# Turned keys and state products of six blocks from one TensorE pass, with every engine's order rewritten

## The chip, the cores and the metric

The kernel runs on one core of a Trainium2 chip. That core has TensorE (PE in the profile: matrix products into PSUM, eight banks of 128 partitions by 512 float32), VectorE (DVE), ScalarE (ACT), GpSimd (POOL, which here mostly starts loads) and SyncE (SP, which starts stores and a few loads). Each engine works through its own instructions in order and waits on semaphores for the others. The metric is the device time of the kernel in microseconds.

## The reference

A linear attention with a decayed state feeds a channel mix. Sizes: batch 4, heads 8, sequence 768, head width 64, so d_model 512; hidden width 1024.

```python
for t in range(S):                       # attention, state is 64x64 for each head
    state = gamma * state + k[t] v[t]^T
    y[t] = scale * q[t] state
x = y, heads side by side                # (4, 768, 512)
x_prev = x, one token later (zeros first)
xk = mu_k * x + (1 - mu_k) * x_prev
xr = mu_r * x + (1 - mu_r) * x_prev
k = relu(xk @ w_k); v = k*k @ w_v        # 512 -> 1024 -> 512
out = sigmoid(xr @ w_r) * v              # w_r is 512x512
```

## The kernel before

The 3072 tokens are cut into 12 blocks of 256 (three to a batch, so blocks 0, 3, 6, 9 begin with an empty state and blocks 2, 5, 8, 11 hand none on). A block's attention is chunked: scores of queries and keys inside the block, a mask, the product with the values, plus the queries times the state carried in. Decay is folded into scale factors of the values and of the output. Blocks 6 to 11 (the tuple HALF, line 17) are cut into four sub-blocks of 64 tokens, so their matmuls are 64x64 tiles of TensorE.

One long string, ORDER, is the program: each word is a piece of work, a number of a block (and more), the PSUM bank after `@` and the engine after `~`. The loop at line 755 emits the words one after the other, and no scheduler changes that. An engine's instructions therefore stand in the order of its own words, and only semaphores tie the engines together. The pieces that matter here, with the lines of the profile:

- `lq`, `lk`, `lv`, `wk`, `wr`, `wv` load (lines 230, 235, 735, 738, 742). Nearly all go through POOL's queue, which casts q, k and the weights to float16. `cq`, `ck` cast the first q and k on ACT (line 241).
- `vs` scales the values to float16 (line 253), on DVE or POOL. The tiles are a ring of three.
- `Tq`, `Tk` turn q and k with transposes against an identity (lines 272 and 278), `Eq`, `Ek` copy the result from PSUM to float16 (line 241, ACT).
- `S` is the scores (lines 318, 331, 339), `M` the masking (lines 347, 354, DVE).
- `C` is the state product k^T v (lines 366, 384, 395), `U` adds it to the carried state (line 419, or a copy at line 241), `G` decays the state into the next block (line 424).
- `I` and `J` are the queries times the carried state (line 441), `Y` the scores times the values (lines 462, 478, 489). All three accumulate in the same PSUM bank pair of a block; `D` scales that into x (lines 507, 514, DVE).
- `t`, `dx`, `X` mix x with its neighbour token (lines 529, 542, 552, 558), `K` is xk times w_k (lines 572, 582), `Qa`, `Qb` relu and square (lines 591, 599, 603, ACT), `R` and `s` the gate and its sigmoid (lines 612, 618), `V`, `O`, `st` the last product, its gating and the store (lines 624, 630, 637). The last half block has its own forms `Vc`, `Oc`, `sc` (lines 642, 649, 657).
- `z` multiplies zeros on TensorE (lines 703, 710) in the start-up.

A key block of 6 to 11 is thus read twice by TensorE before: in `Tk`, 32 transposes of 64 columns into a float16 bank pair, and in `C`, 32 matmuls (24 where no state is handed on) of 64 columns:

```python
nc.tensor.transpose(pt[low(s), u, j, i, :], src[low(u), h, i*D : i*D+D], ident[low(u), low(u)])
nc.tensor.matmul(ps[low(a), u, i, j, :], lhsT=K16(n)[low(u), h, i*D : i*D+D], rhs=VS(n)[low(u), i, h], ...)
```

Of the kernel before, what the change touches and what calls it, by code (L numbers as in the profile page):

```python
# [29 lines left out]
t.0.0.3~a t.0.0.2~a t.0.0.1~a lv.2~p z.2@4 S.1.1@23 M.1.1~v C.1@01 U.1.0~v z.2@4 I.1@23 S.1.0@67  # L30
X.0.0.1~v t.0.1.2~a X.0.0.2~v Tk.2@0 t.0.1.3~a t.0.0.0~a M.1.0~v X.0.0.0~v z.2@4 Y.1 t.0.1.1~a
X.0.0.3~v Ek.2~a K.0.0@0 K.0.1@6 lq.4~p U.1.1~v G.1~a wr~p lk.4~p D.1~v dx.1~v X.1.0.2~v X.1.0.0~v
K.0.2@1 Qa.0.0~a Qb.0.0~a Qa.0.2~a lq.3~p X.1.0.1~v X.1.0.3~v X.1.1.0~v Qa.0.1~a K.0.3@0 Qa.0.3~a
lk.3~p vs.2~v Tq.2@1 X.1.1.2~v K.1.3@6 K.1.0@0 C.2@7 U.2.0~v lv.3~p Eq.2~a S.2.1@23 M.2.1~v S.2.0@45
M.2.0~v Qb.0.3~a lv.4~p K.1.1@1 X.1.1.1~v Qa.1.0~a t.0.1.0~a K.1.2@7 I.2@23 Qb.0.1~a Qa.1.1~a wv.0~p
Qb.0.2~a Tq.4@01 Eq.4~a Y.2 Qa.1.3~a Qb.1.1~a X.0.1.3~v X.1.1.3~v R.1.1@4 Tk.4@01 Ek.4~a J.2 R.1.0@6
Qa.1.2~a s.1.0~a X.0.1.2~v X.0.1.1~v X.0.1.0~v R.0.1@5 s.0.1~a s.1.1~a R.0.0@7 s.0.0~a S.4.1@01
Qb.1.0~a D.2~v dx.2~v X.2.0.2~v X.2.0.0~v S.4.0@23 Tq.3@4 Eq.3~a X.2.0.1~v wv.1~p X.2.0.3~v Tk.3@7
lq.5~p Ek.3~a K.2.2@5 Qa.2.2~a K.2.3@4 M.4.1~v M.4.0~v Qa.2.3~a Qb.2.3~a lk.6~p S.3.1@67 M.3.1~v
S.3.0@01 vs.3~p C.3@23 U.3.0~a Qb.2.2~a K.2.1@4 Qa.2.1~a K.2.0@2 Qa.2.0~a I.3@45 lq.6~p vs.4~v  # L40
C.4@67 U.3.1~v X.2.1.1~v V.0.1.0@3 M.3.0~v V.1.0.0@2 G.3~a U.4.0~v I.4@01 X.2.1.3~v U.4.1~v J.3
Qb.1.3~a Y.4 Qb.2.0~a lk.5~p X.2.1.2~v X.2.1.0~v Y.3 D.3~v dx.3~v V.0.0.0@7 V.0.1.1 O.0.1~v Tq.5@45
J.4 D.4~v dx.4~v R.2.0@6 Qb.2.1~a V.0.0.1 O.0.0~v X.3.0.1~v Eq.5~a Qb.1.2~a V.1.0.1 X.3.0.2~v
O.1.0~v Tq.6@01 Eq.6~a Tk.6@45 Ek.6~a st.0.0~s lk.7~p st.1.0~s V.1.1.0@3 V.1.1.1 O.1.1~v s.2.0~a
R.2.1@0 s.2.1~a lv.5~p X.3.0.0~v X.3.0.3~v Tk.7@67 Ek.7~a G.4~a S.6@45 M.6~v Tk.5@23 Ek.5~a vs.5~v
V.2.0.0@0 K.3.2@1 Qa.3.2~a K.3.0@6 S.5.0@23 M.5.0~v S.5.1@45 C.5@1 U.5.0~v K.3.3@7 Qb.3.2~a Qa.3.0~a
lq.7~p K.3.7@6 Qa.3.3~a Qa.3.7~a lv.6~p lq.8~p vs.6~v M.5.1~v V.2.0.1 st.0.1~s I.5@67 O.2.0~v
st.2.0~s C.6@23 U.6.0~a U.6.1~v U.6.2~v K.3.6@1 Qa.3.6~a lk.9~p X.3.1.3~v Y.5 Tq.7@45 Eq.7~a U.6.3~v
X.3.1.2~v I.6@01 J.5 X.3.1.0~v D.5~v X.3.1.1~v Qb.3.3~a G.6~a V.2.1.0@2 K.3.1@3 V.2.1.1 O.2.1~v
Qb.3.7~a Qa.3.1~a Qb.3.1~a dx.5~v K.3.4@4 K.3.5@5 Qa.3.5~a X.5.0.0~v X.5.0.3~v R.3.1@2 s.3.1~a  # L50
lv.7~p Qa.3.4~a X.5.0.1~v Qb.3.4~a R.3.0@5 R.4.0@2 s.3.0~a s.4.0~a Qb.3.0~a X.5.0.2~v vs.7~v K.5.2@4
S.7@67 st.1.1~s M.7~v Qb.3.5~a Y.6 Qb.3.6~a lv.10~p C.7@23 U.7.0~v X.5.1.1~v Qa.5.2~a K.5.0@5
R.4.1@6 Qa.5.0~a D.6~v s.4.1~a V.4.0.0@4 V.4.0.1 V.3.1.0@5 U.7.1~v Qb.5.0~a X.5.1.3~v U.7.2~v I.7@01
X.5.1.2~v U.7.3~v Tq.8@67 Eq.8~a X.5.1.0~v O.4.0~v lv.8~p vs.8~v Qb.5.2~a lq.10~p lk.8~p Tk.8@23
Ek.8~a V.3.1.1 V.3.0.0@4 C.8@67 O.3.1~v st.2.1~s st.3.1~s Y.7 dx.6~v D.7~v Tq.10@23 V.3.0.1 Eq.10~a
G.7~a dx.7~v X.6.0.2~v V.4.1.0@5 R.5.1@2 s.5.1~a K.5.3@0 Qa.5.3~a R.5.0@2 U.8.0~v O.3.0~v V.4.1.1
lv.9~p lk.10~p lq.9~p Tk.10@01 s.5.0~a U.8.1~v X.6.0.1~v Ek.10~a X.6.0.0~v Tk.9@23 Ek.9~a K.5.1@7
Qa.5.1~a X.6.0.3~v K.6.0@4 lq.11~p Qb.5.1~a Qa.6.0~a U.8.2~v I.8@01 vs.9~v S.8@23 M.8~v O.4.1~v
st.4.1~s K.6.4@7 Qa.6.4~a vs.10~v X.6.1.2~v K.6.2@6 C.9@23 Qa.6.2~a Qb.6.2~a U.9.0~a Y.8 U.9.1~v
D.8~v U.9.2~v U.9.3~v X.6.1.3~v Qb.5.3~a Tq.9@45 V.5.1.0@6 V.5.1.1 O.5.1~v Eq.9~a lk.11~p K.6.3@7  # L60
Qa.6.3~a K.6.7@4 Qa.6.7~a V.5.0.0@7 C.10@45 Qb.6.0~a X.6.1.0~v S.9@23 M.9~v G.9~a Qb.6.3~a Tq.11@01
Eq.11~a V.5.0.1 dx.8~v X.6.1.1~v st.4.0~s K.6.1@6 Qb.6.7~a Qa.6.1~a Qb.6.1~a X.8.0.3~v X.8.0.0~v
U.10.0~v U.10.1~v K.6.5@2 Qa.6.5~a st.3.0~s lv.11~s K.6.6@0 Qa.6.6~a Qb.6.6~a R.6.0@6 s.6.0~a
O.5.0~v U.10.2~v U.10.3~v R.7.0@2 s.7.0~a R.6.1@7 s.6.1~a I.9@45 X.8.0.2~v S.10@23 Tk.11@01 Ek.11~a
X.8.0.1~v K.8.1@7 Qb.6.5~a Qa.8.1~a Qb.8.1~a vs.11~v st.5.1~s K.8.0@6 C.11@01 M.10~v Qb.6.4~a
# [19 lines left out]
def kernel(  # L85
# [114 lines left out]
    def half(n):  # L200
        return n in HALF
# [10 lines left out]
    def first(n):  # L212
        return n % NB == 0
# [586 lines left out]
```

## Time and profile before

| | |
|---|---|
| median of 3 runs | 153.29 us (153.18 to 153.69) |
| span of the profiled execution | 151.4 us, from its first to its last instruction |
| PE busy | 143.4 us, 2426 matmuls |
| DVE busy | 127.8 us, 212 instructions |
| ACT busy | 103.6 us, 195 instructions |
| POOL busy | 55.3 us, 65 instructions |
| granted TensorE clock | 1.000 |

The profiled execution is known by its span; the timed runs count 1.9 us more, which lies around the span. A difference in the span is taken as the same difference in the time. In the view by groups, one row is one line, engine and shape with its count, its busy time and the mean length of one; lengths overlap, since an engine starts an instruction before the one ahead of it has ended, so what an instruction takes of a busy engine is read from one start to the next in the timeline. The chain of waits goes back from the last instruction to what released each step. The view by stretches gives the busy time of each engine between two moments.

### The profile page before, as it was taken

The numbers are of one execution on the slowest core, as the hardware profiler recorded it, in microseconds if no ns is written. First come the engines' busy times: TensorE is split into PE (matmuls) and PEld (weight loads), VectorE is DVE, ScalarE is ACT, GpSimd is POOL, SyncE is SP. The second block draws the span as 40 slices with busy tenths as digits, with TensorE's granted clock in tenths as the row PEclk, the third lists the DMA queues.
The fourth block names the chain that finished last, engine by engine and source line by source line (L and its number), as shares of the span: only waits on it lengthen the run. The fifth ranks groups of instructions, "written<-read, shape, count | busy, mean of one in ns | idle before, by whom it ended". The sixth has DMA issues, their size and how long they took to land.

```text
span 151.4 us, 5541 instructions
## 1 busy us (share of the span) xinstructions
PE 143.4 (95%) x2426; PEld 82.8 (55%) x2426; DVE 127.8 (84%) x212; ACT 103.6 (68%) x195; POOL 55.3 (37%) x65
## 2 busy tenths in 40 slices
PE   7878799999999999999999999999999999999991
PEld 3345487757754554547465564548456444655450
DVE  7886999999989999999999999999799999400432
ACT  3565979899844795779567786999604756839420
POOL 7953998577957309996710000000000000000000
PEclk9999999999999999999999999999999999999999
DMA  5999999999999999999999019301000005500433
GB/s 140 219 229 197 207 231 192 168 251 212 196 167 202 233 262 107 256 300 198 231 173 126 7 38 283 105 35 45 0 4 0 4 0 211 205 0 0 148 133 139
DMA packets 45624, 22.16 MB, mean 146 GB/s; under 512 B 37400, under 2 KB 41248, under 8 KB 45600
## 3 DMA queue, kind: packets, MB, share of 16 engines
q0 software_dynamic: 38704, 14.42, 74.5%
q1 hardware_dynamic: 6592, 7.21, 14.3%
q8 instruction: 19, 0.31, 0.8%
q10 hardware_dynamic: 304, 0.18, 0.4%
q14 instruction: 5, 0.04, 0.1%
HBM read 24.16 MB, written 6.29 MB: 201 GB/s over the span
## 4 chain that ended last, share of the span: by engine, by line
PE 73%; DMA 12%; POOL 11%; issue 1%; DVE 0%; POOLq 0%
PE ps L624 27%; PE ps L572 14%; DMA v<-in_v_dram 12%; PE ps L612 12%; PE ps L582 8%; PE ps L278 3%; POOL q L235 3%; POOL k L230 2%; PE ps L441 2%; POOL vs L253 2%; POOL v L230 2%; PE ps L366 1%; PE ps L462 1%; PE ps L642 1%; PE ps L318 1%
## 5 line engine op out<-in xcount | busy, mean ns | idle before, releaser
L624 PE MATMUL ps<-wv,k2s 128*128 128x512 f16 x184 | 44.1, 380 | 0.0
L591 ACT ACTIVATE kr<-ps 128x512 f32<-128x512 f32 x48 | 27.9, 594 | 12.5 <-PE ps L582 6.5
L624 PEld LDWEIGHTS <-k2s 128*128 128x128 f16 x184 | 17.1, 98 | 18.9 <-ACT k2s L603 0.4
L630 DVE SCALAR_TENSOR_TENSOR os<-ps,rs 128x512 f32<-128x512 f32 x23 | 15.6, 684 | 11.9 <-ACT rs L618 9.4
L612 PE MATMUL ps<-wr,xr 128*128 128x512 f16 x96 | 23.5, 379 | 0.0
L582 PE MATMUL ps<-xk,wk 128*128 128x256 f16 x192 | 23.2, 273 | 0.0
L572 PE MATMUL ps<-xk,wk 128*128 128x512 f16 x96 | 23.0, 379 | 0.0
L618 ACT ACTIVATE rs<-ps 128x512 f32<-128x512 f32 x24 | 13.6, 597 | 12.9 <-PE ps L612 12.1
L230 POOL DMA_DIRECT2D k<-in_k_dram x20 | 17.8, 903 | 10.3 <-PE ps L384 6.7
L582 PEld LDWEIGHTS <-wk 128*128 128x128 f16 x192 | 18.1, 98 | 3.7
L241 ACT COPY qT<-ps 128x1024 f16<-128x1024 f16 (+1 forms) x13 | 12.3, 946 | 9.5 <-PE ps L278 7.8
L558 DVE SCALAR_TENSOR_TENSOR xr<-dx,mu,xT 128x256 f16<-128x256 f32 (+1 forms) x32 | 17.9, 577 | 0.1
L230 POOL DMA_DIRECT2D v<-in_v_dram x18 | 16.0, 911 | 3.6 <-DMA wr<-in_moe_w_r_dram 1.9
L558 DVE SCALAR_TENSOR_TENSOR xk<-dx,mu,xT 128x256 f16<-128x256 f32 (+1 forms) x32 | 17.0, 579 | 0.2
L354 DVE TENSOR_TENSOR a<-ps,c_sb 128x1024 f16<-128x1024 f32 (+1 forms) x14 | 14.6, 1066 | 0.9 <-PE ps L339 0.6
L603 ACT ACTIVATE k2s<-kr 128x512 f16<-128x512 f32 x24 | 14.8, 631 | 0.3
L612 PEld LDWEIGHTS <-xr 128*128 128x128 f16 x96 | 9.0, 97 | 10.7 <-issue 0.5
L572 PEld LDWEIGHTS <-wk 128*128 128x128 f16 x96 | 9.1, 98 | 10.5
L599 ACT ACTIVATE k2s<-kr 128x512 f16<-128x512 f32 x24 | 14.5, 627 | 0.3
L241 ACT COPY kT<-ps 128x1024 f16<-128x1024 f16 (+1 forms) x13 | 12.2, 945 | 2.2 <-PE ps L272 1.7
L529 DVE TENSOR_TENSOR dx<-xT 128x1024 f32<-128x1024 f32 x11 | 13.4, 1221 | 0.2
L253 DVE TENSOR_TENSOR vs<-v,csm_sb 128x1024 f16<-128x1024 f32 x10 | 12.2, 1217 | 0.2 <-DMA v<-in_v_dram 0.2
(73 smaller groups left out, 165.6 us busy)
## 6 DMA issues: line engine op xcount, KB each, us to landing
out_dram<-os SPq DMA_DIRECT2D x23, 256.0 KB, 2.4
v<-in_v_dram POOLq DMA_DIRECT2D x18, 256.0 KB, 7.7
q<-in_q_dram POOLq DMA_DIRECT2D x11, 256.0 KB, 8.4
k<-in_k_dram POOLq DMA_DIRECT2D x21, 128.0 KB, 8.8
v<-in_v_dram POOLq DMA_DIRECT2D x2, 512.0 KB, 7.2
wk<-in_moe_w_k_dram POOLq DMA_DIRECT2D x2, 512.0 KB, 10.4
wv<-in_moe_w_v_dram POOLq DMA_DIRECT2D x2, 512.0 KB, 10.4
wr<-in_moe_w_r_dram POOLq DMA_DIRECT2D x1, 512.0 KB, 8.7
```

What stands on the lines that cost most here:

```text
L230: e.dma_start(out=dst[:, :, i * D : i * D + D], in_=src[:, i * P : i * P + P].rearrange("h p d -> p h d"),)
L241: e.copy(out=out, in_=in_)
L253: e.tensor_tensor(out=VS(n), in0=V32(n).rearrange("p h (i d) -> p i h d", i=2), in1=gks[:, int(half(n) or wide(n)), :, :, None].to_broadca ...
L354: nc.vector.tensor_tensor(out=a_full(n)[:, i, :, j0:j1], in0=pairs(banks("S", n, i, j0))[:, :, j0:j1], in1=(below if wide(n) else causal[: ...
L558: nc.vector.scalar_tensor_tensor(out=XM[w](k)[:, j, t0:t1], in0=DX(k)[:, j, t0:t1], scalar=mu[:, w * NCO + j : w * NCO + j + 1], in1=x[:, ...
L572: nc.tensor.matmul(banks("K", n, g), lhsT=wk16[:, co, g * P : g * P + P], rhs=XM[0](k)[:, co, :], start=(co == 0), stop=(co == NCO - 1),)
L582: nc.tensor.matmul(pz[:, i, :], lhsT=wk16[:, co, fo * P : fo * P + P], rhs=XM[0](k)[:, co, m * TM + t0 : m * TM + t1], start=(i == 0 and c ...
L591: nc.scalar.activation(out=kr, in_=banks("K", n, g, *u), func=AF.Relu)
L603: nc.scalar.activation(out=K2(n)[:, w * g : w * g + w, t0:t1], in_=kr.rearrange("p a t -> p (a t)").rearrange("p (i t) -> p i t", i=w), fu ...
L612: nc.tensor.matmul(banks("R", n, tb), lhsT=XM[1](k)[:, co, t : t + P], rhs=wr16[:, co, :], start=(co == 0), stop=(co == NCO - 1),)
L624: nc.tensor.matmul(banks("V", n, tb), lhsT=K2(n)[:, fo, tb * P : tb * P + P], rhs=wv16[:, fo, :], start=(fo == 0), stop=(fo == NFO - 1),)
L630: nc.vector.scalar_tensor_tensor(out=OS(2 * n + tb), in0=banks("V", n, tb), scalar=1.0 / (KSC * KSC), in1=RS(2 * n + tb), op0=ALU.mult, op ...
```

## The change

For blocks 6 to 11, `Tk`, `Ek` and `C` go. In their place stands `TC`, in two halves `TC.n.0` and `TC.n.1` of 16 matmuls each: the same slice of K is the stationary operand as in `C`, and the moving operand is 128 columns wide, 64 of an identity and 64 of the scaled values. The first 64 columns of the result are the turned keys, the others the state product, both in float32. For that, the tile of scaled values has an identity as its slot 0, written once in the start-up into the three tiles of the ring (three DVE instructions more). `Ec.n.i` copies the turned keys of one half to float16 (ACT, 512 elements of a partition, twice a block; `Ek` was one copy of 1024). `U` reads the state product out of the same banks.

A second new piece, `w`, is a fence: for each of the 12 blocks ACT copies 16 elements of a partition (8 in the first blocks of the whole-block form) out of the bank pair in which `I` has just written. The next matmul that writes there (`J` or `Y`) has to wait for that copy. Before, nothing stood between them.

Besides, the load of w_k is in three pieces (a quarter, a quarter, a half) in place of two halves, the scaling of block 3's values goes from POOL to DVE, the two mu vectors are staged in a tile that also serves output, and ORDER is new throughout, so on every engine and queue pieces stand in other places.

```diff
+MERGED = (6, 7, 8, 9, 10, 11)
 ORDER = """
-cm.0~v cm.1~v cm.2~v gy.0~v mu~a lv.0~p lq.0.0.2~s lk.0.0.2~s ck.0.0.2~a cq.0.0.2~a z.12@6
...
+lq.0.0.2~s cm.0~v mu~a lv.0~p lk.0.0.2~s z.4@2 z.4@3 z.2@2 mt@0 gy.0~v cm.1~v cq.0.0.2~a Tq.0.0.2@1
...
+    def VS(n):
+        return VI(n)[:, 1:].rearrange("p (i h) d -> p i h d", i=2)
+
-    VS = ring("vs_", 3, [2, H, D], F16)
+    VI = ring("vs_", 3, [2 * H + 1, D], F16)
...
-    mu8 = const.tile([P, P], F32, name="mu8")
+    fenced = const.tile([P, 2, NJ, 2], F32, name="fenced")
...
+    mu8 = OS(2)[:, 0:P]
...
+    def both(n, i):
+        return banks("TC", n, i).rearrange("p u (j x t) -> p u j x t", j=NJ, x=2)
+
+    def turned_state(e, n, i):
+        ps = both(n, i)
+        for j in range(NJ):
+            for u in range(2):
+                for a, h, jo, hp in heads(j):
+                    k = 1 + i * H + h
+                    x = slice(0, 2) if more(n) or not (u and i) else slice(0, 1)
+                    nc.tensor.matmul(
+                        ps[low(a), u, j, x], lhsT=K16(n)[low(u), h, i * D : i * D + D],
+                        rhs=VI(n)[low(u), 0 : k + 1 : k][:, x],
+                        start=(j == 0), stop=(j == NJ - 1), skip_group_check=True,
+                    )
+
+    def turned_k_part(e, n, i):
+        copy(
+            e, KT(n)[:, :, i].rearrange("c j (u p) -> c u j p", u=2), both(n, i)[:, :, :, 0],
+        )
...
+        if merged(n):
+            src = both(n, c // 2)[:, c % 2, :, 1]
...
+    def fence(e, n):
+        us = slice(0 if half(n) or not first(n) else 1, 2)
+        e.copy(out=fenced[:, us], in_=pairs(banks("I", n))[:, us, :, 0:C:W])
+
...
-            ((step, 2, ALU.is_ge), (below, 0, ALU.is_ge)),
+            ((step, 2, ALU.is_ge), (below, 0, ALU.is_ge))
+            + tuple((VI(i)[:, 0], 2, ALU.is_equal) for i in range(3) if MERGED),
...
-    def load_wk(e, h):
-        f = slice(h * dff // 2, (h + 1) * dff // 2)
+    def load_wk(e, a, b):
+        f = slice(a * dff // 4, b * dff // 4)
         nc.gpsimd.dma_start(out=wk16[:, :, f], in_=wks[:, :, f])
```

Three places of the new order, on the engines that the prediction speaks of. First DVE in the start-up, from the first scaling of values (tile vs_0) to the first x (tile xT0); a2 is a masked score, tg2 and t32 the carried state. Before:

```order
L253 TENSOR_TENSOR vs_0_74<-v32_0_70,csm_sb_121 128x1024
L354 TENSOR_TENSOR a2_0_83<-ps_61,c16_sb_120 128x2x256
L243 CAST tg2_0_93<-ps_61 128x256
L419 TENSOR_TENSOR t32_0_86<-ps_61,tg2_0_93 128x256
L354 TENSOR_TENSOR a2_0_83<-ps_61,c16_sb_120 128x2x256 x3
L514 TENSOR_TENSOR xT0_130<-ps_61,gy_sb_122 128x2x4x128
```

And now:

```order
L717 TENSOR_SCALAR vs_0_74<-os_3_119,csm_sb_121 128x64
L717 TENSOR_SCALAR vs_1_75<-os_3_119,csm_sb_121 128x64
L717 TENSOR_SCALAR vs_2_76<-os_3_119,csm_sb_121 128x64
L363 TENSOR_TENSOR a2_0_83<-ps_61,c16_sb_120 128x2x256
L262 TENSOR_TENSOR vs_0_74<-v32_0_70,csm_sb_121 128x1024
L363 TENSOR_TENSOR a2_0_83<-ps_61,c16_sb_120 128x2x256
L252 CAST tg2_0_93<-ps_61 128x256
L451 TENSOR_TENSOR t32_0_86<-ps_61,tg2_0_93 128x256
L363 TENSOR_TENSOR a2_0_83<-ps_61,c16_sb_120 128x2x256 x2
L765 TENSOR_TENSOR gy_sb_122<-gy_sb_122,csm_sb_121 128x4x128
L546 TENSOR_TENSOR xT0_130<-ps_61,gy_sb_122 128x2x4x128
```

The three identities are new, one mask stands ahead of the values, and the last power of gy stands behind the masks instead of ahead of the values.

Second, DVE around block 3's values, after the four xk of block 2 (a2 and tg2, t32 as above). Before:

```order
L558 SCALAR_TENSOR_TENSOR xk_2_103<-dx_0_99,mu_125,xT0_130 128x256 x4
L354 TENSOR_TENSOR a2_1_84<-ps_61,c16_sb_120 128x1024 x2
L354 TENSOR_TENSOR a2_0_83<-ps_61,c16_sb_120 128x1024
L253 TENSOR_TENSOR vs_1_75<-v32_0_70,csm_sb_121 128x1024
L419 TENSOR_TENSOR t32_0_86<-ps_61,tg2_0_93 128x256
```

And now:

```order
L594 SCALAR_TENSOR_TENSOR xk_2_103<-dx_0_99,mu_125,xT0_130 128x256 x4
L262 TENSOR_TENSOR vs_0_74<-v32_3_73,csm_sb_121 128x1024
L363 TENSOR_TENSOR a2_0_83<-ps_61,c16_sb_120 128x1024 x2
L451 TENSOR_TENSOR t32_0_86<-ps_61,tg2_0_93 128x256
L262 TENSOR_TENSOR vs_1_75<-v32_0_70,csm_sb_121 128x1024
```

The second row, the values of block 3 (tile vs_0), was POOL's and is DVE's now.

Third, ACT around blocks 9 and 10 (rs is a sigmoid, k2s a square, kr a relu, qT and kT turned queries and keys). Before:

```order
L618 ACTIVATE rs_0_112<-ps_61 128x512
L618 ACTIVATE rs_2_114<-ps_61 128x512
L618 ACTIVATE rs_1_113<-ps_61 128x512
L241 COPY kT_2_82<-ps_61 128x2x8x64
L599 ACTIVATE k2s_111<-kr_2_109 128x2x256
L591 ACTIVATE kr_3_110<-ps_61 128x512
```

And now:

```order
L250 CAST kT_1_81<-ps_61 128x2x4x64
L250 COPY qT_2_79<-ps_61 128x2x4x128
L250 CAST kT_1_81<-ps_61 128x2x4x64
L654 ACTIVATE rs_2_114<-ps_61 128x512
L654 ACTIVATE rs_0_112<-ps_61 128x512
L554 COPY fenced_124<-ps_61 128x16
L635 ACTIVATE k2s_111<-kr_0_107 128x2x256
L654 ACTIVATE rs_3_115<-ps_61 128x512
L554 COPY fenced_124<-ps_61 128x16
```

One copy of turned keys is two now, and the fences of blocks 9 and 10 stand among the sigmoids and squares.

More of the change, by code (lines that the diff above doesn't have):

```diff
@@ L30 @@
[L30 to L65, printed above, removed]
@@ L213, in first, with merged @@
         return n % NB == 0
+    def merged(n):
+        return n in MERGED
     def more(n):
```

91 lines of the change are left out of this document (64 added, 27 removed).

## The prediction

> **What bounds the kernel now.** I read the page's head first, then the view by stretches, cut at the first of TensorE's dense products and at its last matmul.
>
> ```profile
> span 151.4 us, 5541 instructions
> PE 143.4 (95%) x2426; PEld 82.8 (55%) x2426; DVE 127.8 (84%) x212; ACT 103.6 (68%) x195; POOL 55.3 (37%) x65
> ...
> 0.00:19.47 19.47, 15.00 (x314) 8.62 (x314) 15.88 (x43) 11.81 (x24) 14.43 (x20) 1.00 1.30 198
> 19.47:148.26 128.79, 128.36 (x2119) 74.19 (x2112) 111.48 (x170) 91.79 (x171) 40.85 (x46) 1.00 0.85 138
> ```
>
> After the length of a stretch stand PE, PEld, DVE, ACT, POOL, the clock, DMA. From 19.47 on, PE is busy for 128.36 of 128.79 us at full clock. So the span is three things: a start-up of 19.47 us, a stream of PE work of 128.8 us, and a tail of 3.1 us (148.26 to 151.4). The PE timeline (start, length, instructions, idle time before) shows where the stream begins and its one real hole:
>
> ```profile
> 18.79 0.64 PE L489 MATMUL ps<-a,vs 64*64 64x128 f16 x32 [0.28 <-DVE a L354]
> 19.23 0.31 PE L441 MATMUL ps<-qT,tg 64*64 64x128 f16 x8
> 19.47 3.67 PE L582 MATMUL ps<-xk,wk 128*128 128x256 f16 x32
> 23.07 0.64 PE L272 MATMUL ps<-c_sb,q 128*64 128x128 f16 x16
> 23.64 1.95 PE L582 MATMUL ps<-xk,wk 128*128 128x256 f16 x16
> ...
> 37.93 0.44 PE L384 MATMUL ps<-vs,k 128*64 128x64 f16 x16 [0.33 <-POOL vs L253]
> ...
> 148.26 0.02 issue
> 148.28 0.42 DVE os L649
> ```
>
> The last two rows are the end of the chain of waits: PE's last matmul is over at 148.26. The hole is 0.33 us at 37.93: block 3's values, scaled on POOL. DVE is the second bound, from its first x of block 1 (19.78, see below) to the last xr:
>
> ```profile
> 19.78:129.95 110.17, 109.76 (x2004) 63.47 (x2003) 106.87 (x163) 81.71 (x153) 40.54 (x46) 1.00 0.96 147
> ...
> 128.90 0.87 DVE L558 SCALAR_TENSOR_TENSOR xr<-dx,mu,xT 128x256 f16<-128x256 f32 x2
> ```
>
> 106.87 of 110.17 us: only 3.3 us idle. Whatever lengthens DVE's list by more than its slack shows at the end.
>
> **The change, part by part.** *Merged pass.* The groups that it takes away, and the chain of waits for what such matmuls cost in a row:
>
> ```profile
> L278 PE MATMUL ps<-c_sb,k 64*64 64x64 f16 x256 | 3.4, 195 | 0.0
> L366 PE MATMUL ps<-vs,k 64*64 64x64 f16 x176 | 2.7, 195 | 0.0
> ...
> 94.19 0.91 PE ps L624 x4
> 95.09 0.38 PE ps L366 x32
> 95.47 0.26 PE ps L318 x32
> 95.73 0.27 PE ps L278 x32
> ...
> 62.14 0.97 PE ps L624 x4
> 63.11 0.86 PE ps L572 x4
> ```
>
> Inside a run of small matmuls, 32 of 64 columns take 0.27 us. Removed: six `Tk` of 0.27 (1.6 us) and 176 matmuls of `C`, 176/32 x 0.27 = 1.5 us; together 3.1. Added: 192 matmuls, most of 128 columns. The nearest row is line 489, the same 64x64 tiles and 128 columns: 32 from 18.79 to 19.23, 0.44 us. 192/32 x 0.44 = 2.6. Saved: 0.5; 16 of the 192 stay 64 columns wide, but `TC` stands in two halves often apart, so I take 0.4. Bounds: 0 (no cheaper than the two) and 0.7.
>
> [...]
>
> *Fewer switches.* The first small run behind dense products costs 0.38 instead of 0.27 (95.09), and the first dense group behind small ones 0.97 instead of 0.86 (62.14, 63.11): 0.2 us for each excursion. From the first `K` on, PE's words make 25 such excursions before and 23 now: 0.4 us. Bounds 0.2 and 0.6.
>
> *Start-up.* DVE sets when the first `K` can begin, since it makes the xk. Its rows, ACT's first cast, and the loads:
>
> ```profile
> 7.54 1.23 DVE L253 TENSOR_TENSOR vs<-v,csm_sb 128x1024 f16<-128x1024 f32 x1 [0.20 <-DMA v<-in_v_dram]
> ...
> 10.87 1.89 DVE L354 TENSOR_TENSOR a<-ps,c_sb 128x512 f16<-128x512 f32 x3 [0.60 <-PE ps L339]
> 13.95 1.23 DVE L514 TENSOR_TENSOR xT<-ps,gy_sb 128x1024 f32<-128x1024 f32 x1 [1.19 <-PE ps L441]
> ...
> 18.66 0.87 DVE L552 SCALAR_TENSOR_TENSOR xk<-xT,mu,dx 128x256 f16<-128x256 f32 x2
> ...
> 19.78 1.21 DVE L514 TENSOR_TENSOR xT<-ps,gy_sb 128x1024 f32<-128x1024 f32 x1
> ...
> 4.73 0.62 ACT L241 CAST k<-k2s 128x512 f16<-128x512 f32 x1 [2.04 <-DMA k2s<-in_k_dram]
> ...
> k2s<-in_q_dram SPq DMA_DIRECT2D x1, 256.0 KB, 3.1
> k2s<-in_k_dram SPq DMA_DIRECT2D x1, 256.0 KB, 3.5
> wk<-in_moe_w_k_dram POOLq DMA_DIRECT2D x2, 512.0 KB, 10.4
> ...
> 8.12 1.56 POOL L735 DMA_DIRECT2D wk<-in_moe_w_k_dram x2
> 13.66 1.90 POOL L253 TENSOR_TENSOR vs<-v,csm_sb 128x1024 f16<-128x1024 f32 x1 [3.98 <-DMA v<-in_v_dram]
> 15.51 0.95 POOL L235 DMA_DIRECT2D q<-in_q_dram  x1
> ```
>
> Before, q lands ahead of k, yet its cast stands behind k's. Now q is cast first and the first score can be masked while the values are still to be scaled, so most of DVE's waits (0.20 + 0.60 + 1.19 = 2.0 us) have other work in them; I leave 0.4 of them. Against that stand three identities, an estimate of 0.2 each from their row below. So block 1's x comes at 19.78 - 2.0 + 0.4 + 0.6 = 18.8 instead of 19.78, and block 0's at 13.95 - 0.9 = 13.05. On PE the path to the first `K` is then: 13.05, that x (1.15 from start to start), two masks (2 x 1.14), a sum (0.33), `I.1` at 16.9; its fence 0.5, for nothing stands between `I.1` and `Y.1`; `Y.1` with its state part 0.68 (18.79 to 19.47); `Tq.2` and `Tk.2` 1.04. `K` starts at 19.1 and has `Tq.2` (0.57 us, 23.07 to 23.64) behind it: a lead of 0.37 + 0.57 = 0.9. One thing eats of it: half of w_k is now started behind POOL's scaling of block 1's values, at 15.56 and not at 8.9; `K.0.2` wants it at about 21.6. What is ahead of it in the queue decides: before, both halves had landed by 8.9 + 10.4 = 19.3 or somewhat later, now block 2's q is ahead of it as well, so I estimate 22.0. I take 0.5 for the start-up; bounds -1.5 (all of the 10.4 us from 15.56 on, less other waiting) and 0.9.
>
> *Block 3's values on DVE.* The groups that this and the next parts use:
>
> ```profile
> L253 DVE TENSOR_TENSOR vs<-v,csm_sb 128x1024 f16<-128x1024 f32 x10 | 12.2, 1217 | 0.2 <-DMA v<-in_v_dram 0.2
> L241 ACT COPY kT<-ps 128x1024 f16<-128x1024 f16 x11 | 11.0, 1010 | 0.5 <-PE ps L278 0.5
> L591 ACT ACTIVATE kr<-ps 128x512 f32<-128x512 f32 x48 | 27.9, 594 | 12.5 <-PE ps L582 6.5 <-PE ps L572 6.0
> L694 ACT COPY mu<-ps 128x8 f32<-128x8 f32 x1 | 0.2, 183 | 0.0
> L680 DVE TENSOR_SCALAR c_sb<-os,csm_sb 128x64 f16<-128x64 f32 x1 | 0.2, 235 | 0.0
> ```
>
> The hole of 0.33 us goes. DVE gains 1.1 us of list (1217 ns long, 1.13 from start to start). POOL loses 1.9 us ahead of loads.
>
> *Copies.* Six of 1010 ns become twelve of half the size: by line 591, 594 ns from 512 float32 in PSUM, so ACT works 12 x 0.59 - 6 x 1.01 = 1.0 us more, and twelve fences of 0.2 (line 694, 183 ns) are 2.4 us. ACT idles 37 of the 128.8 us after 19.47, and I cost the work at nothing; its place in the order is what can hurt.
>
> *Fences.* A fence costs PE about 0.5 us from the last `I` matmul to the next one in that bank (0.2 of matmul length by the 195 ns of line 366, 0.2 of copy, two hand-overs). Blocks 2, 3, 4, 10 and 11 have dense work of 0.86 or more in between. Blocks 5 to 9 have only small runs, for instance `I.10` and `S.10` for block 9, some 0.4 us; the others 0.5. ACT's word ahead of each fence ends before `I` does if PE runs without holes. I take 0.3 in all; bounds 0 and 3.0 (five times one ACT operation of 0.59 in the way).
>
> *DVE's end.* From 19.78 to the end of the last xr (129.77) its list takes 110.0 us. It now has 1.13 more: 18.8 + 110.0 + 1.13 = 129.9, if it idles as much. The word that needs this last xr is `R.9.0`, and behind it PE has 17 groups of 0.865 and two halves of 0.875, 16.5 us, without further need of DVE's mixing. PE itself arrives there at 148.26 - 1.35 - 16.5 = 130.4. So DVE is in time by 0.5 us, and what saves more on PE than that is cut off there.
>
> **The sum.** 0.4 + 0.4 + 0.5 + 0.33 - 0.3 = 1.3 to 1.35 us off the last matmul; the tail stays (`Vc`, then a copy and a store). A span of 151.4 - 1.35 = 150.05. The median of the runs stands 1.89 above the span, and the same difference gives 153.29 - 1.35 = 151.9 us.
>
> **The rivals.** *DVE takes the gain.* For: 97% busy, more list. If its waits of 2.0 us in the start-up stay as they are, x of block 1 comes at 20.4, and the last xr at 131.5; the end is 131.5 + 0.1 + 16.5 = 148.1 instead of 148.26: 153.1 us, no change. Against: the waits were for work that is now earlier. Chance 0.17.
>
> *The fences stall PE*, the other side: five of them (5 to 9) are covered by 0.4 to 0.55 us only, and each copy stands behind sigmoids, squares and relus of 0.6 us. One such operation late at each is 5 x 0.59 = 3.0 us, 151.9 + 3.0 = 154.9. It decides from 0.27 us a fence (1.35 over five), and makes it clearly slower from 0.36. For: no trace shows a fence, and what is late on PE makes ACT late too. Against: ACT has a quarter of its time free. Chance 0.21.
>
> *The merged pass is dear*: the identity and the values lie apart, and if that breaks the four-fold overlap, the nearest row is line 272's 16 two-tile transposes of 128 columns in 0.47 (0.57 less one switch), 29 ns each: 192 x 29 = 5.6 us, 2.5 more than removed, 151.9 + 2.9 = 154.8. Against: line 489's 14 ns for the same tiles. Chance 0.07. [...]
>
> *More gain*: start-up 0.9 and free fences, 151.9 - 0.7 = 151.2, where DVE's end limits. Chance 0.05.
>
> **How the numbers follow.** My forecast, 151.9, has 0.50, with its own range of 151.0 to 152.8 (start-up and merged pass at their bounds). About 0.3% either way, 152.83 to 153.75, is what counts as no change. Faster: 0.50 + 0.05 + half of the first rival = 0.63. No change: the other half and a little of the third, 0.11. Slower: 0.26. The range for 8 in 10 leaves out the worst of the fences and of the merged pass: 151.0 to 154.3.
>
> **What the profile after would show.** Right: the first dense group at about 19.1; the merged groups at 13 to 15 ns from start to start; the copies of turned keys near 590 ns; no idle time of PE behind line 554; the last xr near 130; the last matmul near 146.9. Wrong: PE waits on ACT's fences or on w_k; 29 ns a merged matmul; DVE idle by over 5 us between block 1's x and the last xr, with `R.9.0` waiting for it.

## The result, and the profile after

The changed kernel takes 158.52 us (median of 4 runs, 157.18 to 159.85), beside 153.31 for the kernel before on the same chip: a ratio of 1.026 (95% interval 1.023 to 1.029). My forecast was 151.9, faster; it is slower, and outside my range of 151.0 to 154.3. This ratio, like those below, leaves out executions over 1.5% longer than the fastest of the same kernel, here two of the four, near 159.8 us with a granted clock of 0.978. The profiled one took 157.26 us, with a span of 155.5 us where before had 151.4; the sums below are against these two spans.

The head of the page after, the view by stretches cut as in the prediction (first dense product to last matmul), and the rows of the PE timeline from 17.5 us on that have idle time over 0.2 us:

```profile
span 155.5 us, 5242 instructions
PE 144.9 (93%) x2254; PEld 82.3 (53%) x2254; DVE 128.9 (83%) x216; ACT 104.1 (67%) x213; POOL 54.1 (35%) x65
...
19.42:152.37 132.95, 128.37 (x1924) 73.34 (x1920) 111.53 (x169) 92.21 (x187) 38.62 (x45) 1.00 0.84 135
...
17.72 0.64 PE L521 MATMUL ps<-a,vs 64*64 64x128 f16 x32 [0.28 <-ACT fenced L554]
...
76.90 1.04 PE L660 MATMUL ps<-wv,k2s 128*128 128x512 f16 x4 [2.50 <-issue]
79.42 2.75 PE L660 MATMUL ps<-wv,k2s 128*128 128x512 f16 x12 [0.29 <-DVE os L666]
83.64 1.92 PE L618 MATMUL ps<-xk,wk 128*128 128x256 f16 x16 [1.48 <-issue]
...
136.60 1.02 PE L648 MATMUL ps<-wr,xr 128*128 128x512 f16 x4 [0.24 <-ACT kr L627]
```

The stream begins where it did before (19.42, before 19.47). PE is busy in it for 128.37 us, before 128.36. But it now lasts 132.95 us instead of 128.79: it stands still for 4.58 us where it stood still for 0.43. Nearly all of that is two holes, 2.50 us ahead of 76.90 and 1.48 us ahead of 83.64, and both are put down to "issue": the profile shows nothing that PE waited for. From the start of one matmul to the start of the next they cost 4.3 us (the ends of matmuls are modelled), and the span grew by 4.1.

The new work itself came out close to its price. Here are the groups of the merged pass, the new copies and the fences:

```profile
L422 PE MATMUL ps<-vs,k 64*64 64x128 f16 x176 | 4.6, 219 | 0.0
L250 ACT CAST kT<-ps 128x512 f16<-128x512 f32 x12 | 6.9, 596 | 2.4 <-PE ps L422 1.8 <-DVE tg L451 0.7
L554 ACT COPY fenced<-ps 128x16 f32<-128x16 f32 x10 | 1.8, 175 | 7.9 <-PE ps L473 7.9
```

One thing besides looked like a cause at first: VectorE waits 3.3 us for a store.

```profile
74.12 1.22 DVE L356 TENSOR_TENSOR a<-ps,c_sb 128x1024 f16<-128x1024 f32 x1
78.67 0.69 DVE L666 SCALAR_TENSOR_TENSOR os<-ps,rs 128x512 f32<-128x512 f32 x1 [3.34 <-DMA out_dram<-os]
...
64.60 1.02 SPq L239 DMA_DIRECT2D v<-in_v_dram x2
65.67 22.07 SPq L673 DMA_DIRECT2D out_dram<-os  x5
```

The result of block 4 (`O.4.1`) needs a buffer that the store `st.2.1` has to empty, and in the new order that store stands on SyncE's queue behind block 11's values (`lv.11`), two loads of 256 KB. I had not read SyncE's queue in the new order at all. So there were two theories. A: the load of block 11's values is at fault, by the store behind it or by its bytes in a crowded stretch. B: the merged pass, the fences or the new order as such are.

### The profile page after: what moved, and what is told of

It reads as the page before. It is cut to its first block, busy times and chain, and to the rows that moved or that the text cites. A ratio compares the mean times of both kernels' runs of the same rounds, so it can differ in the third digit from the quotient of the medians.

```text
span 155.5 us, 5242 instructions
## 1 busy us (share of the span) xinstructions
PE 144.9 (93%) x2254; PEld 82.3 (53%) x2254; DVE 128.9 (83%) x216; ACT 104.1 (67%) x213; POOL 54.1 (35%) x65
## 3 DMA queue, kind: packets, MB, share of 16 engines
q0 software_dynamic: 39232, 14.42, 74.1%
## 4 chain that ended last, share of the span: by engine, by line
PE 63%; DMA 13%; ACT 10%; DVE 5%; issue 4%; POOL 2%; SPq 1%; DVEq 0%; ACTq 0%; POOLq 0%
PE ps L660 22%; PE ps L618 11%; PE ps L648 10%; DMA out_dram<-os 8%; PE ps L608 6%; ACT kr L627 5%; DMA k<-in_k_dram 5%; ACT k2s L635 3%; PE ps L473 2%; PE ps L281 2%; PE ps L510 1%; PE ps L340 1%; DVE xT L546 1%; PE ps L287 1%; PE ps L678 1%
## 5 line engine op out<-in xcount | busy, mean ns | idle before, releaser
L660 PE MATMUL ps<-wv,k2s 128*128 128x512 f16 x184 | 43.4, 379 | 2.8 <-issue 2.5
L618 PE MATMUL ps<-xk,wk 128*128 128x256 f16 x192 | 23.7, 273 | 1.5 <-issue 1.5
L608 PE MATMUL ps<-xk,wk 128*128 128x512 f16 x96 | 22.1, 379 | 0.0
L262 DVE TENSOR_TENSOR vs<-v,csm_sb 128x1024 f16<-128x1024 f32 x11 | 13.3, 1216 | 0.0
L244 POOL DMA_DIRECT2D q<-in_q_dram x12 | 10.6, 885 | 2.7 <-PE ps L287 1.3
```

The costliest lines, as they stand in the source:

```text
L608: nc.tensor.matmul(banks("K", n, g), lhsT=wk16[:, co, g * P : g * P + P], rhs=XM[0](k)[:, co, :], start=(co == 0), stop=(co == NCO - 1),)
L618: nc.tensor.matmul(pz[:, i, :], lhsT=wk16[:, co, fo * P : fo * P + P], rhs=XM[0](k)[:, co, m * TM + t0 : m * TM + t1], start=(i == 0 and c ...
L660: nc.tensor.matmul(banks("V", n, tb), lhsT=K2(n)[:, fo, tb * P : tb * P + P], rhs=wv16[:, fo, :], start=(fo == 0), stop=(fo == NFO - 1),)
```

## First experiments: the store is not it

All of these are against the kernel before beside them, 153.21 us (7 runs).

**late_v11**: after, with `lv.11` moved far back on SyncE's queue, so that no store stands behind it until 108 us.

```
- ... Qb.3.5~a lv.11~s Tq.9@45 ...
+ ... V.6.0.0@7 lv.11~s st.5.0~s ...
```

Block 11's values are scaled here before they are loaded, so block 11 of the output is not the reference's; the instructions and their sizes are the same.

> The changed kernel with one word moved: the load of block 11's values (lv.11) leaves its place on SP's queue ahead of the store of block 2's second half and stands ahead of the first store of block 5, near 118 us, when few other loads run. Theory A (the load holds up the store behind it, DVE waits 3.3 us for that store's landing, and the same 512 KB in a crowded stretch make TensorE's own instruction loads late, its two holes of 2.5 and 1.5 us without a visible releaser): all three waits go, the span falls from 155.5 to about 151.3 us, the time to 153.0 to 153.6. Theory B (the holes belong to the merged pass, the fences or the new order as such): no more than 0.5 us comes off, 156.7 or more.

Measured: 156.95 us, ratio 1.022 (1.017 to 1.027). The store wait of 3.3 us is gone, and the holes of PE have stayed:

```profile
77.26 1.04 PE L660 MATMUL ps<-wv,k2s 128*128 128x512 f16 x4 [2.86 <-issue]
83.46 0.72 PE L618 MATMUL ps<-xk,wk 128*128 128x256 f16 x5 [1.27 <-issue]
```

Their sum was 3.98 and is 4.13 us. So VectorE's wait lay beside a standstill of PE and was not the loss, and the time is where theory B had it.

**store_first**: after, with `st.2.1` put ahead of `lv.11`.

> The changed kernel with the store of block 2's second half put ahead of the load of block 11's values on SP's queue, which keeps its place otherwise. Theory A1 (the order on the queue is what counts: the store is stuck behind the load): DVE's wait of 3.3 us at 75 us goes, and the time falls by 2.5 to 4 us to 153.2 to 154.8. Theory A2 (the load's bytes in the crowded stretch are what counts, through the instruction loads): the holes of PE of 2.5 and 1.5 us that no releaser explains stay, and the time stays above 156.

Measured: 159.34 us, ratio 1.037 (1.031 to 1.044). The store wait is gone again and the time has not fallen, so the order on SyncE's queue is not the loss either. The first hole is longer still, and ahead of the second border there is none:

```profile
78.44 1.89 PE L660 MATMUL ps<-wv,k2s 128*128 128x512 f16 x4 [3.43 <-issue]
...
78.40:84.00 5.60, 5.57 (x121) 2.97 (x122) 1.57 (x3) 2.66 (x7) 0.00 (x0) 0.50 1.46 215
```

The second row, of the view by stretches, shows as its third number from the end that the granted clock was 0.50 in the 5.6 us behind the hole. The four value products at 78.44 take 1.89 us in it, in after 1.04 (76.90): the work up to the next border lasts longer. More on that below.

**before_early_v11**: the kernel before, with `lv.11` put as early as after has it, ahead of a store (`st.1.1`, about 70 us).

> The kernel before with one word moved: the load of block 11's values goes from 91 us to the same kind of place that the changed kernel has, right behind block 7's scaling of values (near 70 us) and ahead of the store of block 1's second half on SP's queue. Theory A (load in the crowded stretch, stores behind it): DVE waits for the landing of that store before block 3's second result (77.8 us), PE has holes in 74 to 86 us, and the kernel is 2 to 5 us slower, 155.3 to 158.3. Theory B (the change's other parts are at fault): within 0.5 us of 153.3.

Measured: 157.61 us, ratio 1.028 (1.025 to 1.031).

```profile
81.92 0.69 DVE L630 SCALAR_TENSOR_TENSOR os<-ps,rs 128x512 f32<-128x512 f32 x1 [4.21 <-DMA out_dram<-os]
...
82.67 1.02 PE L624 MATMUL ps<-wv,k2s 128*128 128x512 f16 x4 [2.45 <-DVE os L630]
```

So the placement of that load is dear by itself: in a kernel without the large holes PE waits for VectorE, which waits for the store, and the profile says so. The wait of 2.45 us is not all of the 4.4: from 83.93 to 87.34 us the granted clock is 0.50, another 1.7. In after the same fault is there and is hidden behind holes with another cause. Mending it could not show until these are gone.

**late_v11_split**: late_v11 with every merged matmul of 128 columns as two of 64, so that 176 matmuls more run (with the same remark on block 11).

> As late_v11, but each merged matmul of 128 columns is two of 64 columns, one against the identity and one against the values, at the same place, with the same PSUM layout and the same copies. By the rows of the trace (32 matmuls of 64 columns 0.27 us, 32 of 128 columns 0.44) PE has 6 x 0.10 = 0.6 us more work: 0.3 to 0.7 us slower than late_v11. [...]

Measured: 159.75 us, ratio 1.041 (1.037 to 1.045), 2.8 us above late_v11, where I had thought of 0.3 to 0.7. This miss was the key. The added work is 0.6 us, as priced; 1.6 are longer holes (5.70 us together, 4.13 in late_v11), and 0.4 a later first key product. The holes are still there, but in other pieces of work, and in the middle of them:

```profile
75.98 0.25 PE L327 MATMUL ps<-qT,kT 64*64 64x64 f16 x8 [3.25 <-issue]
...
82.45 0.35 PE L423 MATMUL ps<-vs,k 64*64 64x64 f16 x18 [2.45 <-issue]
```

A score pass of 32 matmuls stands still after 24 of them. No data explains that: all 32 read the same tiles. What the two kernels have in common is the count. The view by stretches, from 0 up to the moment ahead of each hole, gives in brackets behind PE and PEld how many matmuls and weight loads have started; first of after, then of the split kernel:

```profile
0.00:76.89 76.89, 71.49 (x1246) 42.32 (x1246) 71.74 (x125) 57.37 (x117) 54.06 (x65) 1.00 1.48 208
0.00:83.60 83.60, 76.46 (x1374) 44.94 (x1374) 76.36 (x131) 60.03 (x124) 54.06 (x65) 1.00 1.51 206
```

```profile
0.00:75.90 75.90, 69.84 (x1246) 41.26 (x1246) 69.59 (x122) 55.14 (x114) 54.03 (x65) 1.00 1.50 207
0.00:82.40 82.40, 73.86 (x1374) 43.90 (x1374) 73.83 (x127) 59.82 (x124) 54.03 (x65) 1.00 1.49 203
```

1246 and 1374 in both, 128 matmuls apart, each with its weight load: 256 instructions. That points to the instructions themselves. The page's list of DMA queues has a queue for them, and narrow windows of that view show when a piece comes in (packets, MB, share of the 16 engines' time in the window; the windows are 71.3 to 74.5, 74.5 to 75.6, 76.9 to 81.1 and 81.1 to 82.2 of after, the second and fourth with a piece):

```profile
q8 instruction: 17, 0.28, 0.7%
...
q0 software_dynamic: 1729, 0.40, 131.6%
...
q0 software_dynamic: 573, 0.11, 116.9%
q8 instruction: 1, 0.02, 5.1%
...
q0 software_dynamic: 3883, 0.57, 191.5%
...
q0 software_dynamic: 731, 0.09, 133.3%
q8 instruction: 1, 0.02, 5.1%
```

17 pieces for 2254 matmuls: 0.28 MB / 17 = 16 KB a piece. Counted from 1246 in steps of 128 both ways, the borders lie at 94 + 128 n; 17 of them are below 2254, and 19 below the 2426 of the kernel before, whose page has 19 pieces. One piece is moved between 74.5 and 75.6, and PE goes on at 76.90; the next between 81.1 and 82.2, and PE goes on at 83.64. Between them no instructions come in, while the packets of GpSimd's queue (q0) add up to more than the whole time of the 16 engines.

The trace gives the size (one packet of 16 KB for 128 matmuls with their weight loads) and how far ahead a piece comes: the packet ahead of matmul 1246 begins at 74.57 us, 3.3 us after matmul 1118, the first of the piece before it, has started (71.3).

**Theory H**, then: a piece of 256 instructions is asked for when the piece before it is entered. In after the piece from matmul 1118 is entered at 71.3 us and the next one is usable at 76.90, 5.6 us later; the following takes 83.64 - 76.90 = 6.7. The work inside must last that long, or PE stands still. The new order puts `I.6`, `Tq.9`, `S.7` and `Y.6` side by side there, 120 small matmuls in 1.2 us. First the stretch of after from the entry on, then the one of before from the same count, 1118, to 1246:

```profile
71.28:74.30 3.02, 3.02 (x133) 2.25 (x132) 2.92 (x5) 2.75 (x6) 2.35 (x3) 1.00 1.66 172
```

```profile
64.72:70.98 6.26, 6.26 (x128) 3.42 (x129) 6.02 (x10) 5.31 (x11) 5.05 (x7) 1.00 1.36 242
```

After has used up some 130 matmuls in 3.0 us (the stretch's end counts a few that overlap it), before took 6.3 us for 128.

## Experiments on the instruction pieces

Two ways to test H: move the borders of the pieces without touching the work, and free the DMA engines without touching PE. The runs of before beside these three: 153.37 us (13 runs).

**before_pad48**: the kernel before, with 48 small matmuls of zeros at 46 us.

```
- ... Tq.5@45 J.4 D.4~v dx.4~v R.2.0@6 ...
+ ... Tq.5@45 J.4 D.4~v dx.4~v n.48@6 R.2.0@6 ...
+ nc.tensor.matmul(banks("n", count)[low(a), 0:8], lhsT=z16[low(u), 0:D], rhs=z16[low(u), 0:8], ...)
```

> Kernel before with 48 more matmuls that do nothing useful (64x8 zeros, two tiles in turn) in front of the gate's first product of block 2 (46 us). Theory H (TensorE's instructions come in pieces of 16 KB, 128 matmuls with their weight loads; each piece is fetched while the one before it runs, and 5.5 to 6.5 us go by from entering a piece to having the next while loads crowd the DMA engines, 3 us afterwards): the pieces' borders move 48 matmuls earlier in the work. By the trace of before, read with the borders so moved, four pieces get too short for their fetch: holes that end in front of the trace's matmuls number 862 (2.2 us, at 49.5 us), 990 (1.8 us, at 55.4), 1374 (0.6 us, at 80) and 1502 (3.1 us, at 84), each with no releaser; span 151.4 + 7.7 = about 159, and the time 3 to 5% longer even where part of it is made up. Rival R1 (the holes come from what the pieces of work wait for, and the order of the work alone decides them): no new hole, 48 matmuls more, 0.5 to 1 us: 153.7 to 154.3, ratio 1.003 to 1.007.

Measured: 162.36 us, ratio 1.057 (1.054 to 1.061): 48 matmuls, 0.9 us of work, cost 9.0 us. These are all idle rows over 0.4 us behind 20 us, the counts ahead of them, and the granted clock behind each hole:

```profile
51.86 0.38 PE L278 MATMUL ps<-c_sb,k 64*64 64x64 f16 x24 [1.71 <-issue]
86.50 0.43 PE L278 MATMUL ps<-c_sb,q 64*64 64x64 f16 x16 [2.74 <-issue]
...
0.00:51.80 51.80, 45.16 (x862) 29.59 (x863) 47.54 (x88) 36.28 (x69) 38.53 (x46) 1.00 1.51 203
0.00:86.40 86.40, 77.06 (x1502) 46.44 (x1503) 76.99 (x131) 58.48 (x110) 55.26 (x65) 0.98 1.40 197
...
51.86:56.50 4.64, 4.64 (x36) 1.79 (x35) 0.86 (x3) 1.51 (x2) 0.00 (x0) 0.63 1.26 263
86.50:91.00 4.50, 4.50 (x29) 1.92 (x29) 3.10 (x7) 1.97 (x5) 0.00 (x0) 0.63 0.05 10
```

Of the four holes that H gave, the two large ones are there, in front of the matmuls it named (862 and 1502), in the middle of transposes, 1.7 and 2.7 us long where I said 2.2 and 3.1. The other two (1.8 us at 990, 0.6 at 1374) did not come; I take it that the first hole, which moves all work behind it, gave their fetches time, which no run tests. That the work or its order alone decides is refuted: here both are those of before. The span grew by 9.0 us (160.4), and 8.8 of it add up: holes 4.45, the added work 0.9, and behind each hole a granted clock of 0.63, (4.64 + 4.50) x 0.37 = 3.4. Cut more narrowly, the clock is 0.50 for 3.41 us behind each (52.24 to 55.65 and 86.38 to 89.79).

**after_held**: after, with the last four loads of GpSimd's queue held until block 7's x is written. **late_held**: the same, and `lv.11` late but ahead of its use.

```
- lv.10~p K.6.5@7 U.8.1~v lq.11~p ... lk.9~p ... lq.10~p ... lk.11~p lk.10~p
+ lv.10~p lk.9~p h.7~p lq.10~p lk.10~p lq.11~p lk.11~p K.6.5@7 ...
+ def hold(e, n): e.tensor_copy(out=held_at, in_=x[:, 0, c : c + 1])
- ... lv.11~s Tq.9@45 ...              (late_held only)
+ ... st.4.0~s lv.11~s s.7.0~a ...
```

> Kernel after with the last four loads of GpSimd's queue (queries and keys of blocks 10 and 11, 1 MB of tiles, 2 MB read) held until block 7's x is written (about 79 us in after): a small copy on GpSimd stands in front of them. Nothing else is moved but the first half of block 9's keys, which goes ahead of them. Theory H: with these loads gone the DMA engines are free by about 70 to 74 us, a piece of instructions is there 3 to 4 us after the one before it is entered, and the two holes of TensorE (2.5 us in front of matmul 1246, 1.5 us in front of 1374) shrink to less than 1 us together. What may then be bare is VectorE's wait for a store that stands behind block 11's values on SyncE's queue (3.3 us in after, hidden), itself shorter since the load ahead of it lands sooner. Time 154.5 to 156.5, ratio to before 1.008 to 1.02. Rival R1: holes as in after, in front of the same pieces, 157 to 159. Rival R3 (a hole is needed in any case since 128 small matmuls take 1.2 us whatever the DMA does): holes of 2 us or more remain.

Measured: 156.95 us, ratio 1.015 (1.012 to 1.019): the ratio is inside H's range, the median 0.45 us above it. Its profile is of an execution of 158.14 us, and in it a hole of 3.87 us still stands ahead of matmul 1246. From 71.5 to 76.2 us GpSimd's packets take 76% of the engines' time there and those of SyncE's loads and stores 66%; so holding the four loads does not remove the hole in every execution.

> The same with block 11's values loaded behind the second store of block 4 on SyncE's queue, ahead of their first use, so that no store stands behind a load. Theory H with the store's wait as the second cost: neither hole nor store wait; what is left is the change as it was forecast, 151.4 to 154, ratio 0.99 to 1.005. If the held version alone is as fast, the store's wait was not bare. Rival R1: 156 to 158.

Measured: 154.05 us (10 runs), ratio 1.0044 (1.0026 to 1.0063), at the upper end of the range (154, 1.005). From late_v11 (1.022) to late_held it is 2.9 us, and the change is on GpSimd's queue alone, apart from the place of block 11's values. The PE timeline where the holes were, the DMA queues from 72.6 to 74.1, and the two rows with idle time that are left behind 20 us:

```profile
73.72 1.05 PE L619 MATMUL ps<-xk,wk 128*128 128x256 f16 x8
74.60 1.89 PE L661 MATMUL ps<-wv,k2s 128*128 128x512 f16 x8
76.42 0.33 PE L474 MATMUL ps<-qT,tg 64*64 64x64 f16 x16
...
80.22 1.91 PE L619 MATMUL ps<-xk,wk 128*128 128x256 f16 x16
...
q0 software_dynamic: 461, 0.06, 60.3%
q8 instruction: 1, 0.02, 4.0%
...
22.70 0.62 PE L341 MATMUL ps<-qT,kT 64*128 64x128 f16 x15 [0.74 <-issue]
133.18 1.02 PE L649 MATMUL ps<-wr,xr 128*128 128x512 f16 x4 [0.24 <-ACT kr L628]
```

The eight value products at 74.60 run through the place where after stood still for 2.5 us, and the key products at 80.22 follow without the 1.5. The loads take 60% of the engines' time in that stretch, in after 117 to 191%. Two smaller losses are left: a hole at 22.70, behind 351 matmuls, one past a border (94 + 2 x 128 = 350), and a wait for ScalarE at 133.18.

**late_held_bank**: late_held with one key product of block 11 in a bank that ScalarE does not read just then (`K.11.1@0` becomes `K.11.1@4`).

> late_held with one key product of block 11 (group 1) put into PSUM bank 4 instead of bank 0, where the gate's last product of block 9 waits for ScalarE to have read it (0.24 us idle and a slower first matmul, 0.4 us in all, at 136 us of after). If that wait is on the path to the end: 0.3 to 0.5 us less than late_held, 153.6 to 153.8, ratio 0.999 to 1.003. If ScalarE's next reads are what the end waits for: no change, 154.0.

Measured: 153.54 us (12 runs), ratio 1.0014 (0.9985 to 1.0042), before beside it 153.29 (17 runs). That is 0.5 us below late_held, as expected, though the two intervals overlap; the wait for ScalarE at 133 us is gone from the profile.

**held_shifted** and **held_shifted2**: late_held_bank with all borders 83 matmuls earlier in the work, by small matmuls of zeros in the start-up, to be rid of the hole at 22 us.

```
- z.4@3 z.2@2 mt@0      /  Ek.0.0.2~a z.3@3 S.0.1.0.2@45
+ n.87@3 mt@0           /  Ek.0.0.2~a n.86@45 S.0.1.0.2@45
```

> late_held_bank with the borders of the instruction pieces moved: at the very start, where TensorE still waits for the first queries, 87 matmuls of 64x8 zeros stand in the place of two fillers, so that every border falls 83 matmuls earlier in the work. Theory H: late_held still has a hole in front of matmul 351 (0.74 us at 22 us, no releaser) and an earlier one of up to 0.6 us in front of 222 (2.1 us from the fetch's start to the first matmul); with the borders moved the trace of late_held gives 0.4 us of stall in their place, in front of what was matmul 266. Time 1.0 us below late_held_bank if nothing else ends the start-up (its first key product stands at 19.9), 0.3 us below if the wait for block 1's data takes over: 152.6 to 153.4, ratio 0.993 to 1.0. Rival R1 (borders do not matter): the same as late_held_bank within 0.2 us, or 0.5 us slower by the 87 matmuls (1.5 us of work for 1.4 us of fillers).

> held_shifted moved the borders but took away 2 us of the wide fillers at the start, and TensorE then ran its first matmuls at half speed up to 15 us. Here all fillers of the start stay but one (three matmuls of 512 columns, 0.82 us at 5.8 us), and 86 matmuls of 64x64 on all four quarters, 8 ns each by the rows of the half blocks, stand in its place: 0.7 us for 0.8. The borders fall 83 matmuls earlier, as there. Theory H: first key product near 19.5 as in after, no hole at 22 us and at most 0.5 us of stall near 74: 152.6 to 153.2 where late_held_bank has 153.5, ratio 0.994 to 1.0. [...]

Both missed. held_shifted took 156.19 us (1.018, 1.012 to 1.023). A hole of 1.45 us stood ahead of matmul 1246 (74.81), and the start ran slow: three fillers of 512 columns, the same instructions as in after, first after, then held_shifted:

```profile
5.76 0.82 PE L747 MATMUL ps<-zero 128*128 128x512 f16 x3
```

```profile
6.69 1.46 PE L752 MATMUL ps<-zero 128*128 128x512 f16 x3
```

So with 87 matmuls of 64 by 8 in the place of the two wide fillers, these three take 1.46 us, in after 0.82: from start to start 0.40 to 0.43 us each, in after 0.22. The next ones, at 11.3 us, run at 0.22 again (two in 0.59 us; the expectation of held_shifted2 says 15 us, which is too late). The granted clock of this execution is 1.000; why its start is slow was not shown. The first key product came at 21.0 us, in late_held_bank at 20.1.

held_shifted2 kept the other fillers, and they ran as in after (0.82 us for the three at 6.89 us). But its first key product came at 20.7 us, behind a wait of 1.21 us for block 1's keys, it took 156.73 us (1.021, 1.018 to 1.024), and the hole was back:

```profile
75.70 0.59 PE L328 MATMUL ps<-qT,kT 64*64 64x64 f16 x27 [2.62 <-issue]
...
0.00:75.60 75.60, 68.95 (x1246) 41.24 (x1246) 69.67 (x122) 55.43 (x114) 48.87 (x59) 1.00 1.44 201
```

Matmul 1246 again, in yet another piece of work, now in the middle of a score pass. With the borders earlier in the work, the piece before it was entered at 68.9 us, and there the loads still took 135% of the DMA engines' time (68.9 to 73.4; in late_held 12% from 73 to 76). I had priced that entry as if they were free. The mechanism held, the place in time was wrong.

**held_less4**: late_held_bank with four fillers fewer in the start-up (`z.3@3` twice, `z.5@1` and `z.3@7` each one less), so that each border falls four matmuls later in the work.

> late_held_bank with four fillers fewer at the start (four of the 512-column matmuls of zeros, 1.1 us of filling by 0.27 us each, all in time in which TensorE waits for data), so that each border of the instruction pieces falls four matmuls later in the work. Theory H: the piece that holds the 128 small matmuls at 72 to 75 us then holds four value products more (0.9 us), which is longer than the 3.3 us that the next piece needs from the entry (1.0 to the fetch, 2.3 to its first matmul, by the trace of late_held_bank): no hole in front of matmul 1246, where late_held_bank has 0.6 to 0.8 us. Nothing else changes: 152.7 to 153.1, ratio 0.996 to 0.999. Rival (that idle time is ScalarE's squaring, as the profile puts it down): the hole stays with the value product, in front of matmul 1242: the same time as late_held_bank, 153.5. A cold start as in held_shifted would show as a first key product after 20 us.

Measured: 153.24 us (12 runs), ratio 1.0002 (0.9982 to 1.0023). The pair of rows shows what moved, first late_held_bank, then held_less4:

```profile
76.06 1.04 PE L661 MATMUL ps<-wv,k2s 128*128 128x512 f16 x4 [0.61 <-ACT k2s L640]
...
0.00:76.00 76.00, 71.59 (x1246) 42.26 (x1246) 71.83 (x125) 57.37 (x117) 48.82 (x59) 1.00 1.42 200
```

```profile
73.95 1.89 PE L661 MATMUL ps<-wv,k2s 128*128 128x512 f16 x8
76.22 0.33 PE L474 MATMUL ps<-qT,tg 64*64 64x64 f16 x16 [0.38 <-issue]
...
0.00:76.20 76.20, 71.55 (x1246) 42.33 (x1246) 72.29 (x126) 57.48 (x117) 48.88 (x59) 1.00 1.42 199
```

The four value products in front of which late_held_bank stood still (put down to a square of ScalarE there) now run on with the four ahead of them, and the rest of the hole, 0.38 us, stands four matmuls later, ahead of number 1246 again. So it was never the square: the releaser that the profile names can be a work that merely ended close by. I had said that the hole would go wholly and the time come to 152.7 to 153.1; neither did, since this fetch took 1.9 us to begin (71.9 to 73.8), not 1.0.

This is the fastest version of the change; the runs can't tell it from the kernel before. None of them beats before.

The traces tie the holes together. Behind 15 us, the twelve kernels other than before show 17 idle times of PE of 0.2 us or more that are put down to "issue", and the one of 0.61 us put down to ScalarE. Each of the 18 ends 1.3 to 1.6 us after a packet of the instruction queue has landed, and that packet began only 1.4 to 4.9 us after the piece before it was entered; in after the two packets begin at 74.57 and 81.18 us, 3.3 and 4.3 us after that, and take 0.89 us each, and PE goes on 1.4 and 1.6 us later. Before has no such idle time.

What was not tried: a version without the fences. Before has none, and no run here shows what they guard against. What they cost is read from the trace alone: 0.28 us of waiting, at block 1, where before waits as long for VectorE.

## Why the prediction was wrong, step by step

The step that failed is the first, "PE is busy for 128.36 of 128.79 us", and what the sum made of it: every term was a difference of work or of one wait, and the stream was taken to stay as closed as it was. The sum has no term for the supply of instructions, and no rival had a standstill of PE without a releaser; the runs showed 4.3 us of it. The old stream had no holes because its instructions came in time, and that was a property of the old order: between 23 and 85 us before takes 6 to 8.6 us for the 128 matmuls of a piece, where after has one of 3.0 us. What I could have seen: 2426 matmuls and 19 instruction pieces in the old trace, and in the new order a run of four small pieces, 120 matmuls, with nothing dense between them.

- *Merged pass* (0.4): right. From start to start of the matmuls, `Tk` and `C` of blocks 6 to 11 took 3.84 us and the 192 merged ones 3.48: 0.36 saved. Both terms of the sum (3.1 and 2.6) were 0.7 to 0.9 too small, and their difference held. The rival "the merged pass is dear", 29 ns a matmul, did not come about: it is 18 (3.48 / 192). The four-fold overlap that it names shows from start to start: 128 columns take 14 ns on the 64x64 tiles of line 489, 29 on two tiles (after, 16 from 18.40 to 18.87) and 56 for line 582 on 128x128 (before, 32 of 256 columns from 19.47 to 23.07).
- *Start-up* (0.5): right in size, 0.3 late in its steps. Block 1's x came at 18.91 (forecast 18.8), the first key product at 19.42 (forecast 19.1, before 19.47); with block 2's turned queries, 0.52 us, now ahead of it, that is 0.57.
- *Fewer switches* (0.4) and *block 3's hole* (0.33): not found. The wait for POOL is gone, but what is left of the small pieces takes 0.1 us more than before from start to start, where 0.73 less was forecast, 0.3 of fences against it. A price per switch from two rows did not carry over to the whole order; why is open.
- *Fences* (-0.3): 0.28 us of waiting for a fence in all, at block 1, where before waited 0.28 us for VectorE. The rival "the fences stall PE", 154.9, is refuted.
- *DVE's end*: not tested in after, where PE was late. In late_held the last xr ends at 129.8 (forecast 129.9), and no product of the gate waits for it. The rival "DVE takes the gain" did not come about.
- *Copies at nothing*: nearly right; one product of the gate waits for ScalarE at 136.60, 0.4 us from start to start, and moving one bank took that away.
- *Not in the sum at all*: the instruction pieces, 4.3 us, and the load ahead of the stores on SyncE's queue, 0.36 us here (79.42), 4.4 when put into before.

Together: -0.36 - 0.57 + 0.1 + 0.3 (the dense products with that wait) is about 0.5 us of gain, where 1.35 were forecast, and 4.3 + 0.36 against it: 4.1 us more, which is the span's growth.

## What to carry to other kernels

When a reordering puts many small matmuls side by side, count them against time: here PE gets 128 matmuls with their weight loads per fetch, and from entering one piece the next takes 5.6 to 6.7 us in after under full DMA load, 3.7 in late_held_bank with the last loads held. An idle time of PE with no releaser that stays at the same count of instructions while the work is changed points to a late fetch (here ahead of matmul 1246 in after, late_v11_split, held_shifted2 and held_less4); an instruction packet that lands shortly ahead of its end, here by 1.3 to 1.6 us, confirms it. Adding or taking away a few instructions early in the program moves it, so a kernel can lose several per cent (5.7 in before_pad48) by a change that has nothing to do with the work at that place. Read every queue for a load that has come to stand ahead of a store, and mend it even where the profile shows it hidden: by itself it cost 4.4 us in before_early_v11.

## What was not expected of the hardware

- 48 matmuls of zeros, 0.9 us, cost 9.0 us in the kernel before (162.36 against 153.37 us).
- A hole costs more than its length where the clock falls behind it: 0.63 over 4.6 us behind one of 1.71 us, 0.50 over 5.6 us behind one of 3.43 us, and no drop behind after's 2.50 us or late_v11_split's 3.25 us in the profiled executions. So the length of the hole alone does not decide it.
- Which engine the profile names as releaser can be wrong when the cause is a fetch: 0.61 us put down to a square of ScalarE moved with the count of instructions, not with the square, and shrank to 0.38.
